# Logits stored by position, offset and head, with one GpSimd product for the V products of two positions

## The chip, the cores and the metric

The kernel runs on one core of one Trainium2 chip (trn2). The core has a matrix engine (TensorE, PE in the profile, with its weight loads as PEld), a vector engine (VectorE, DVE), a scalar engine (ScalarE, ACT), GpSimd (POOL) and SyncE (SP), which here only issues transfers. Data stands in on-chip memory with 128 partitions (SBUF) or in the matrix engine's accumulator banks (PSUM); transfers between them and main memory are called DMAs and are issued by SP, ACT and POOL. The metric is the device time of one execution in microseconds, as the median of the runs.

## What is computed

The reference mixes two branches of the same kind of input, 2048 positions of 640 channels, by a gate for each position.

```python
# branch A: 32 heads of 20 channels, each position looks at 8 positions, 2 apart, behind it
idx = pos[:, None] - off[None, :]                 # off = 0, 2, ..., 14
logits = jnp.einsum("bhsd,bhswd->bhsw", q, kg) * scale
logits = jnp.where(mask[None, None, :, :], logits, -1e9)   # mask = idx >= 0
attn = _softmax(logits, axis=-1)
o = jnp.einsum("bhsw,bhswd->bhsd", attn, vg)
a = o.transpose(...).reshape(B, S, D) @ wo
# branch B: a product in the frequency domain
b = irfft2(rfft2(B_x) * (w_r + 1j * w_i))
g = _sigmoid((x * gate_w).sum(-1, keepdims=True))
return g * a + (1 - g) * b
```

## The kernel before

**Layout.** Position s is 16 p + j: partition p has 16 neighbouring positions. As the heads look back in steps of two, even and odd positions never meet, and every stage runs for a parity `par` (8 even or 8 odd positions of a partition).

**Stages.** The projections to q, k and v (`qkv`) run on PE for each parity and each group of 8 heads; every 128 x 480 result is three exact products in a split format (15 matmuls), copied out by ACT and stored to main memory (`qkvd`). `fold` and `cols` begin the spectral branch on DVE, POOL and PE. `attend(par, h)` makes the attention of 4 heads (80 channels) and one parity, 16 times in all, entirely without PE: it loads kt, q and vt for the 8 positions and the 7 before them. `freq(g)` runs 16 frequency groups: ACT lays out zc, PE multiplies (v, u), DVE adds (ab), PE multiplies again (x, z), ACT issues two transfers that exchange halves (`P<-X`), POOL multiplies P by the weights and adds, DVE finishes (z, s), PE transforms back (g), and ACT copies into zg. `project_even` multiplies the even positions' attention by wo, `spatial` takes the spectral branch back, `project_odd` finishes the odd positions.

**One `attend`** (lines 510 to 570), with the names as they stand in the profile (a suffix 6a is head group 6, first half): for each of four pairs of positions, a product pr of kt and q (1280 elements; on DVE with q first copied by ACT into PSUM, `qbank`; in ten of the sixteen, the last pair's product on POOL) and a sum over the 20 channels into L. Then ACT writes -1e9 into the places before the first position (`mask`, one partition), DVE takes the maximum m, POOL subtracts it, ACT takes the exponential, DVE sums to s and inverts, POOL multiplies. Then, again for each pair, POOL makes the V products pv, one instruction for each position, 640 elements each, and DVE sums over the 8 offsets into o, which is stored.

L is kept as position, head, offset: the 8 offsets of a head lie side by side. The maximum and the sum over the offsets read L densely. A V product takes vt (8 offsets of 80 channels, contiguous), each weight repeated for the head's 20 channels, and writes pv as channel, offset, that is with a step of 8 elements.

**Order.** All instructions are first recorded (`Plan.record`) and then issued in a stored order: `ORDER` (line 204) is a compressed list of places, and `Plan.order` takes the operations out of the recorded list one by one by it. Each engine runs its own instructions in that order and none passes another, so an instruction that waits holds everything behind it on its engine; a DMA issue is such an instruction too. Most tiles stand in rings (`Ring`) with two to eight places, and a tile's first writer waits for the last reader of what stood there.

Nearly all instructions are issued from one line and show as L385 in the profile; they are told apart by the names of their tiles.

Of the kernel before, what the change touches and what calls it, by code (L numbers as in the profile page):

```python
# [12 lines left out]
ALU = mybir.AluOpType  # L13
AX = mybir.AxisListType
# [221 lines left out]


# [18 lines left out]
class Mixer:  # L256
# [253 lines left out]
    def attend(self, par, h, step=4):  # L510

        p, d = self.p, self.qkv_d
        V, A, G, S = p.dve, p.act, p.pool, p.sp
        u, f = 4 * par + h // 2, h % 2
        nm = f"{u}{'ab'[f]}"
# [30 lines left out]
        for square in ((4, 1, 0, 1), (2, 4, 4, 2), (1, 2, 6, 4)):  # L546
            self.mask(L, *square)
        m = self.mr.next(f"m{nm}", 8, 4)
        V.tensor_reduce(out=m, in_=L, axis=AX.X, op=ALU.max)
        G.tensor_sub(L, L, m.unsqueeze(3).broadcast_to([128, 8, 4, 8]))  # L550
        A.activation(out=L, in_=L, func=AF.Exp, scale=SCALE)
        s = self.sr.next(f"s{nm}", 8, 4)
        V.tensor_reduce(out=s, in_=L, axis=AX.X, op=ALU.add)
        V.reciprocal(s, s)
        G.tensor_mul(L, L, s.unsqueeze(3).broadcast_to([128, 8, 4, 8]))
        yield
        for jj in range(0, 8, 2):
            if jj % step == 0:
                o = self.orr.next(f"o{nm}{jj}", 4, HC)[:, 0:step]
            pv = self.pvr.next(f"pv{nm}{jj}", 2, HC, 8)  # L560
            for i in range(2):
                G.tensor_mul(
                    pv[:, i].rearrange("p (h d) r -> p r h d", d=HD),
                    vt[:, jj + i : jj + i + 8].rearrange("p r (h d) -> p r h d", d=HD),
                    L[:, jj + i].rearrange("p h r -> p r h").unsqueeze(3).broadcast_to([128, 8, 4, HD]),
                )
            V.tensor_reduce(out=o[:, jj % step : jj % step + 2], in_=pv, axis=AX.X, op=ALU.add)
            if jj % step == step - 2:
                self.queue("o").dma_start(self.o_d[par][:, jj + 2 - step : jj + 2, HC * h : HC * h + HC], o)
                yield  # L570
# [396 lines left out]
```

## Time and profile before

| What | us |
|---|---|
| median of 3 runs (lowest, highest) | 453.96 (453.48, 454.35) |
| the profiled execution | 455.89 |
| its span, first to last instruction | 454.1 |
| PE busy | 441.2 (97%) |
| DVE busy | 409.8 (90%) |
| POOL busy | 363.9 (80%) |
| ACT busy | 211.9 (47%) |
| the 16 products P<-P,wp on POOL | 35.4 |

The granted clock of PE is 0.996 of full speed. Busy time is the union of an engine's instructions, and matmuls overlap, so PE's share says little by itself; how many matmuls start in a stretch says more. A row of a group gives the engine, the operation, the tile written and those read, the shapes and the count, then the busy time and the mean of one in ns, then the engine's idle time ahead of them and who ended it. A row of the timeline gives the start, the duration, and in brackets the idle time ahead. Neighbouring instructions of POOL and DVE overlap a little in their records, so that what one instruction holds its engine for is read from start to start.

### The profile page before, as it was taken

What the parts mean: (1) busy time and instruction counts of PE and PEld (TensorE: products, weight loads), DVE (VectorE), ACT (ScalarE), POOL (GpSimd) and SP (SyncE); (2) the same over time, 40 slices, a digit from 0 to 9 for tenths busy, and PEclk for the clock granted to TensorE, in tenths of its full rate; (3) what the DMA queues carried; (4) which work ended last, traced back from release to release, by engine and by line L of the source; (5) the groups of instructions that cost most, each with busy time, mean ns of one, the idle gap of its engine ahead of it and who ended that gap; (6) DMA issues with size and microseconds to landing.
All of it is one profiled execution on the core that took longest, in us unless ns stands there. A gap on an engine that the chain in (4) does not pass through costs nothing. (4 is left out here: it accounts for less than half of the span.)

```text
span 454.1 us, 7249 instructions
## 1 busy us (share of the span) xinstructions
PE 441.2 (97%) x2440; PEld 391.8 (86%) x2440; DVE 409.8 (90%) x519; ACT 211.9 (47%) x561; POOL 363.9 (80%) x316
## 2 busy tenths in 40 slices
PE   9999999999999999999998989999989999999996
PEld 6888888888889888899886769998877899999996
DVE  4899999899999999999978989999999997899484
ACT  4723165625226463255356666667554655342110
POOL 1158895899899898988977898976899998889810
PEclk9999999999999999999998999999999999999999
DMA  8998999887968979679979778989883331365932
GB/s 312 401 383 268 340 330 377 305 264 237 272 183 272 340 217 316 181 216 320 303 220 294 240 230 250 297 245 320 258 257 105 85 97 54 118 207 134 296 123 87
DMA packets 73956, 110.75 MB, mean 244 GB/s; under 512 B 21296, under 2 KB 50992, under 8 KB 73920
## 3 DMA queue, kind: packets, MB, share of 16 engines
q1 hardware_dynamic: 40192, 69.32, 46.8%
q10 hardware_dynamic: 32816, 36.97, 26.1%
q0 software_dynamic: 912, 4.00, 2.4%
q8 instruction: 19, 0.31, 0.3%
q14 instruction: 17, 0.14, 0.1%
HBM read 72.51 MB, written 32.84 MB: 232 GB/s over the span
## 5 line engine op out<-in xcount | busy, mean ns | idle before, releaser
L385 PE MATMUL qkv<-w,xo 128*128 128x480 f32 (+1 forms) x480 | 110.6, 385 | 0.0
L385 PE MATMUL qkv<-w,xe 128*128 128x480 f32 (+1 forms) x474 | 104.3, 382 | 0.0
L385 PEld LDWEIGHTS qkv<-w,xe 128*128 128x128 f32 x474 | 89.3, 189 | 15.2 <-ACT xe L385 0.9
L385 PEld LDWEIGHTS qkv<-w,xo 128*128 128x128 f32 x480 | 89.7, 189 | 13.8 <-ACT zg L385 0.2
L385 ACT COPY ev<-qkv 128x480 f32<-128x480 f32 x64 | 34.9, 558 | 48.3 <-PE qkv L385 35.9
L385 PE MATMUL woa<-wo,oT 128*128 128x320 f32 x240 | 47.2, 318 | 0.4 <-ACT oT L385 0.4
L385 PE MATMUL wob<-wo,oT 128*128 128x320 f32 x240 | 46.9, 315 | 0.2 <-ACT ya L385 0.2
L385 POOL TENSOR_TENSOR P<-P,wp 128x963 f32<-128x963 f32 (+1 forms) x16 | 35.4, 2212 | 6.6 <-DMA P<-X 4.0
L385 PEld LDWEIGHTS woa<-wo,oT 128*128 128x128 f32 x240 | 37.7, 188 | 1.1 <-ACT oT L385 0.6
L385 PEld LDWEIGHTS wob<-wo,oT 128*128 128x128 f32 x240 | 37.8, 188 | 0.6 <-ACT ya L385 0.4
L385 POOL TENSOR_TENSOR fx<-fx 128x160 f32<-128x160 f32 (+1 forms) x16 | 12.8, 818 | 24.2 <-DMA fc<-in_t_fc 17.1
L385 POOL TENSOR_TENSOR w<-raw,w 128x480 fp32r<-128x480 f32 (+1 forms) x20 | 24.8, 1262 | 5.3 <-ACT w L385 5.3
L385 ACT CAST oT<-oTp 128x384 fp32r<-128x384 f32 (+1 forms) x32 | 13.4, 427 | 30.9 <-PE oTp L385 17.3
L385 PEld LDWEIGHTS g<-mm,s 128*128 128x128 f32 x150 | 21.0, 190 | 7.1 <-ACT zg L385 5.0
L385 PE MATMUL g<-mm,s 128*128 128x128 f32 x150 | 23.5, 280 | 3.1 <-ACT zg L385 3.0
L385 DVE TENSOR_TENSOR oT<-oTp,oT 128x384 fp32r<-128x384 f32 (+1 forms) x32 | 15.2, 485 | 11.0 <-ACT oT L385 10.7
L385 PE MATMUL oa<-gt,zg 128*128 128x161 f32 (+1 forms) x96 | 24.0, 344 | 0.0
L385 PE MATMUL ob<-gt,zg 128*128 128x161 f32 (+1 forms) x96 | 22.0, 344 | 0.0
L385 PE MATMUL u<-bt,zc 128*128 128x240 f32 (+2 forms) x96 | 21.1, 335 | 0.7 <-DVE ab L385 0.7
L385 PE MATMUL v<-bt,zc 128*128 128x240 f32 (+2 forms) x96 | 21.5, 335 | 0.2
L385 DVE TENSOR_TENSOR fx<-fx 128x642 f32<-128x642 f32 (+2 forms) x24 | 19.2, 798 | 0.7
L385 PEld LDWEIGHTS u<-bt,zc 128*128 128x128 f32 x96 | 16.9, 199 | 2.9 <-PE g L385 0.9
(304 smaller groups left out, 1107.6 us busy)
## 6 DMA issues: line engine op xcount, KB each, us to landing
qkvd<-ev ACTq DMA_DIRECT2D x32, 480.0 KB, 4.8
wp<-in_ws SPq DMA_DIRECT2D x16, 642.0 KB, 5.9
raw<-in_wqkv SPq DMA_DIRECT2D x25, 240.0 KB, 5.9
fx<-in_x SPq DMA_DIRECT2D x8, 641.0 KB, 7.9
ot<-od SPq DMA_DIRECT2D x16, 320.0 KB, 3.9
P<-X ACTq DMA_DIRECT2D x30, 160.5 KB, 4.6
fd<-fx POOLq DMA_DIRECT2D x6, 640.0 KB, 5.6
f<-fd SPq DMA_DIRECT2D x6, 640.0 KB, 6.1
```

Of the source, the lines that this page charges most:

```text
L385: p.dve.memset(w, 0.0)
```

## The change

It does four things.

L is declared as position, offset, head (8, 8, 4). The sum of the K products now writes 32 neighbouring values for each position, and the mask writes the same elements at their new places.

The maximum and the sum over the offsets read L through a view that puts the offsets innermost again, so with a step of 4 elements. The factors m and s of POOL's two operations on L are repeated over the middle axis instead of the last one.

The two V products of a pair of positions become one of 1280 elements. vt is read through a view whose two positions overlap (positions jj to jj+7 and jj+1 to jj+8), and because offset and head now lie side by side, the weights of two positions are one run of 64 values, each repeated 20 times. The 128 instructions become 64.

The stored order is another one. Beside the 64 operations that are gone, 101 stand elsewhere in their engine's list: 8 on PE, 21 on DVE, 48 on ACT, 13 on POOL, 11 on SP (the fewest that turn the one list into the other).

```diff
-        L = self.Lr.next(f"L{nm}", 8, 4, 8)
+        L = self.Lr.next(f"L{nm}", 8, 8, 4)
...
             V.tensor_reduce(
-                out=L[:, jj : jj + 2].rearrange("p j h r -> p j r h"),
+                out=L[:, jj : jj + 2],
                 in_=pr.rearrange("p j r (h d) -> p j r h d", d=HD),
...
-        V.tensor_reduce(out=m, in_=L, axis=AX.X, op=ALU.max)
-        G.tensor_sub(L, L, m.unsqueeze(3).broadcast_to([128, 8, 4, 8]))
+        V.tensor_reduce(out=m, in_=L.rearrange("p j r h -> p j h r"), axis=AX.X, op=ALU.max)
+        G.tensor_sub(L, L, m.unsqueeze(2).broadcast_to([128, 8, 8, 4]))
         A.activation(out=L, in_=L, func=AF.Exp, scale=SCALE)
         s = self.sr.next(f"s{nm}", 8, 4)
-        V.tensor_reduce(out=s, in_=L, axis=AX.X, op=ALU.add)
+        V.tensor_reduce(out=s, in_=L.rearrange("p j r h -> p j h r"), axis=AX.X, op=ALU.add)
         V.reciprocal(s, s)
-        G.tensor_mul(L, L, s.unsqueeze(3).broadcast_to([128, 8, 4, 8]))
+        G.tensor_mul(L, L, s.unsqueeze(2).broadcast_to([128, 8, 8, 4]))
...
-            for i in range(2):
-                G.tensor_mul(
-                    pv[:, i].rearrange("p (h d) r -> p r h d", d=HD),
-                    vt[:, jj + i : jj + i + 8].rearrange("p r (h d) -> p r h d", d=HD),
-                    L[:, jj + i].rearrange("p h r -> p r h").unsqueeze(3).broadcast_to([128, 8, 4, HD]),
-                )
+            w = vt[:, jj : jj + 8]
+            w = bass.AP(tensor=w.tensor, offset=w.offset, ap=[w.ap[0], [HC, 2], [HC, 8], [1, HC]])
+            G.tensor_mul(
+                pv.rearrange("p j c r -> p j r c"),
+                w,
+                L[:, jj : jj + 2].rearrange("p j r h -> p (j r) h").unsqueeze(3).broadcast_to([128, 16, 4, HD]),
+            )
...
-            tensor=ap.tensor, offset=ap.offset + first, ap=[ap.ap[0], [31 * step, n], [32, size], [8, 4], [1, size]]
+            tensor=ap.tensor, offset=ap.offset + 4 * first, ap=[ap.ap[0], [28 * step, n], [32, size], [1, 4], [4, size]]
```

Of the moved operations these are spoken of further on, each in its engine's list:

- ACT: the first copy of q6b to qbank stands ahead of the load of vt6a (it stood behind it); the load of q6b stands two operations and a store later. For the groups 3, 13 and 15 a copy from g to zg that stood behind both loads P<-X stands ahead of them (3) or between them (13, 15). The conversion of the first weight block w0 stands behind two of the five loads issued at the start, where it stood behind all five.
- POOL: the V products of the last pair of 6a and the first of 6b stood split around and behind P11; now 6b's first stands between P11's product and its addition, and 6a's last behind them. The subtraction of the maximum from L5a stands ahead of P12 (it stood behind). The store of zero rows into qkvd stands behind the folds 0 to 2 (it was the first).
- SP: the loads of wo and of the table fct stand earlier, the loads kt5b and kt4b later.

More of the change, by code (lines that the diff above doesn't have):

```diff
@@ L233 @@
-%-FB#M0Qq%ICg_IFP2C48|n56Sm9Um9k2fiPvpqah%)KEUW1~=uV*6=QB*z{Al8lvW9Q;ye=6Tp=v>L79H5IQ5X|z~#8hpnJr+Ga_QrkC4`Rhv7#WXovCK>ybSs8B6l~NOoIP)O5Fr!S
-+}fcYgLx<p#v>wbK=gW?vhdCXZVtgKhsHNHj%~Qolp5+lQ(hjj51#p5_1_2~j|^=(cHJD!9j9&qpZdcxvk%!cXv8;;W{9m%oyJFbB38c|mac656_T8#{}Kg@00
+T>t<81poj4|NsC0{{R31`zHT$$W25WFW#<Ufx}n*nCNU>g@m450OU8>60Nx$Gb89Hl9P1EN2FO}PCCgfdlknEb|e<rai~6a6Gj7t(`^GCh}-Zq0%Nht>e4N4i=1^+C0-pl#~%f%Wq7Mx
+E@|Z1eo=ly=Q4UtCR(E^lMWpq_%;YWs{yxs@@IJ$GIZ6M2sMkb@2|PFhrJngjX(ycmYm3qsU`*g%&K%Bpzz1rHj7QjB>RD3mG!7CtjzFVdyzIKiIG7Cx?{RMlS`CG1mEp0=&j)6A?X*v
@@ new lines @@
+iBB3+!_RL+20IIcT&+?<I{Hrgqd-p9!)D$L8Bdl)ddc(4w2+8neyWg&TsF>LH<+59h;unr(b{%ktR-D2#u5E^kry-q6Y>S!m>>=K>(8HQHp2<eAIpXL7#$Z@U^f@WdcB+21k5EEIWwI%
+H*6Chp!sZ&$dWLX=gg`R+aQxu;q)IVEpvGC<5}IMQLT|Diuz{6fBQEhc@!?`Tx+~3US8`S2WP;S9&%i0=T<`p3;7IL5q&0}hGPc~XpCPfzhMr}10X`ETd0oXV*lg*)BM4I6trbc-Jd%v
+&*_B0BEtIm&X|odr<hDKAagh}+lKEzN9i0mLg`L8ycb?vG0|f}*-{%1ek?c<U9pNjY9g;BQW!^#l?w56#$IAz`Mtq}cNi}^oFNjJ-~CwRGqV*vw0L(V_H^}e3NEp{+=WJ2hO!rv*rWGD
+kZV&Mh6LOOcBdmX-}LYBcGvvrUNE>3OLn}mhv=sy(KQJpeVe6bJ()!^#YHL&6ZN;oeG#?lU<Ab&OHux6U}Su#_~4i!^hMZobA#o&^>sD95+YY;q=4}{hel3tBj;(@h)6uLcP@UhAu8Cm
@@ new lines @@
+&2UMC;dDoLt4>q-+<~U$kRmaaaTuWPWzg?k-Lf5x$#>G2`zWxQGes!@;f1|f=R3HF<3OU9{q)S*Mz=ZH>5=(&hVX#UNzU~Z*sYEg*9WNblIt3?9Jr}2qzi4!CIgTN&3AP?0M4eM4x9qh
+l@*$u3)2=4jA|~}Kee=35WO=}Jg&V-Ywl|$(8F<iSj3meYbfy@V97-A1Bd(*cQuW+h8*#JWjncI!*wkAhI@h+OZ;1iT(*n)Y22HmBUJTl>vf%hJut)QATDe9{mcW(kBl+Oi*M)%ZCjBR
+*H~Jys^=hlj@hm7(#J2allRq9KL?1E@G3D`Y=@Gx3X|AGq9|M?avl^+%!=BC)ESD^GgjkriG^YDKm$nN69I8Qw2U;6<|#a!V7aR%k`27#7$~|onH*T&JOX_LT6PxEVdexeHHl-lBpaz%
+4>zBR!u#c-q!SrNkg6g$Y10;|>1=wDC&&Y`j>e%klG@b`u>G4l9|6a5_9bi05Yp@cwyQs1wY0U}PCkA_uI9{WkAG9N+GfiGhvL+U#$B6AGCa~H5ZsAVE?LU&a7FokIxiIUk8?}24<*Tk
@@ new lines @@
+a^|PjtsVEK6d%$A3g0jIRS_e)PY&IlT3=*PI3fePV)MLuZ}>Hvy)8b^1_|K66)cp`wGMXdbpWOV-AYF79<HMgcv9*V^xErSx#5_<I|w64h>rKqQO%lLON^%<;<QVwlyMU$OwEOz(C>nt
+&d;N!tC|@Q_8PNnoaea>Ie770JC?;M1p)v8_UJY=*CE|IjY-%(O7uueoeDZLyi!QyedJop8`)qgl}kfXknrMa^&2fT+>Ni-ViT68@gr9yr(f!s1UyzwIvn>ij9!Qe61w9Q`xACDqoEo9
++LzxYFEL>8b&{sq1Tmi6DBV4_7pFxLh2>jn;)g-{{;>b~tMy?vyK7wiiPZ6_9p;#YAw64cz%nt;y(Lf~k;rGyL_)GG_KTX5CJq-vk|MnGy6&QGr93_WTDK>3>l}miXm3`24>D#p1e28=
+C17SjrIGwlHk_156UD07b%(<Z%RO4GsVO5Q-1%)<D9UBopX~HyZi>`5tuJ|+azwKzysbl=Knv2``=>KCE5G)l8}mshVfS|P7&^u}1wLxZ&pj#6ty1D0qFTqJ?0S8?q1Ux`!M9XHIic6{
@@ new lines @@
+M6YAMaF58qg}a&XoSdUbNiN~#zM49SwwB6?iDkQS2zx7`XB?KEm)H?9IaKmF_emPS{92_=c7`fuE3nxNi6ftZ#-0tPFlDMs)P>3dp#{|>jtC4alz~g-wQOE9u(#=s_MchYWqTP_hKGsc
+q)-MKaJ*bW;uul9bOhvr{w%<`*cYn>XEcE+xRx32r^z~QS``t8Z^<yGW94kW3|s~N51IaK1&Lb3;!uyEdfT6c`gGp%;R@c|!|)(pFk<w)u5i43rFkc?cuOQ2ccgBznPJxsnlm>b*?4Q#
+-}s!$-?FzKN=k15D~R7CqQJgn-&1LlxV0iC8kVGuTYcFx^PWr8QoEDUKecXWjFuMuwHrAdb?AIiUtmWkEypE+5f@2>n9*-x+Dhn9JxNeh>^6kEOaDx$@YIf_Z{!#=88A1~>Z%hhblCu4
+wSYRS4Xp!CV9T>a|D`*i%p_h%_p&xtiwncj|NWZ0)1owoRY_!+q7r;d`!R2*EMy75mn>U$`~kvOb%We<Ae_U=&HfFU*66$<BsU{1ahiOnlQLWfvO3(MN`N^<lhhUKy0<owWM8CMB?^F<
@@ L235 @@
+Tep_ZV@M0f!s`~1o)A2MydHLre-aXK^oDftbXMtsc<jO%H=p*CT}vsQ$vN;s<Z&4ijQ6X{(OP+UG9_DX10A5Ac^bmo|7Put&0sMkl~H}$eDz$=#1V`^qdDV7D)fvB>MJY`=G3k1|I*)w
+Dvn0C6Yy|3z9S=UJ<-SSR}(%!?;6byKX#n?)SRoIJs%@Bfgp-dhS*04!=GsPqX%=S+9P-`cgqlRJ*%R~fm&@*HJs7A%LgZ-<Tis44fd-c-skR}wORGN2!1s<yn>eS1`vqQj}mN||C?(N
+0T!7G4;V!$#r}{A-<2fLg`#Esa$I`C2`X8!wM)Nk6v0eQgl1e0O7)Rpn)CVw+eK{|uO!g|0=3!gA(}fsUZ<PVSKdgv1Q}lcedN;s
 """
```

36 lines of the change are left out of this document (8 added, 28 removed).

## The prediction

> **What bounds the kernel now.** I read the windows first, since a mean over the span mixes stages, and then the waits of TensorE.
>
> ```profile
> 75.00:100.00 25.00, 25.00 (x116) 21.60 (x115) 23.48 (x23) 11.01 (x29) 23.05 (x19) 1.00 0.85 285
> 125.00:150.00 25.00, 25.00 (x136) 22.19 (x135) 24.83 (x22) 11.70 (x31) 25.00 (x19) 1.00 0.76 242
> 225.00:250.00 25.00, 22.88 (x108) 19.37 (x107) 20.57 (x27) 13.68 (x43) 19.21 (x17) 0.93 0.86 257
> 250.00:275.00 25.00, 22.29 (x129) 18.92 (x128) 22.94 (x37) 16.59 (x49) 22.93 (x19) 1.00 0.78 236
> 325.00:350.00 25.00, 22.50 (x141) 19.48 (x142) 24.26 (x34) 12.21 (x34) 24.27 (x19) 1.00 0.72 217
> 375.00:400.00 25.00, 25.00 (x160) 23.16 (x159) 19.87 (x35) 10.64 (x27) 21.99 (x19) 1.00 0.35 110
> 425.00:454.00 29.00, 25.19 (x176) 24.88 (x175) 16.50 (x40) 3.21 (x8) 7.59 (x9) 1.00 0.43 143
> ```
>
> The columns are the busy microseconds of PE, PEld, DVE, ACT and POOL, then the granted clock and the DMA. Up to 225 us PE is never idle: 116 matmuls of 480 columns in 25 us are one in 0.2155 us. What DVE and POOL do there, the attention in the background, is nearly full too (24.83 and 25.00 of 25), but a microsecond saved in it shortens nothing by itself. Idle PE stands in three of these windows: 2.12, 2.71 and 2.50 us, together 7.3 us. Behind 350 us PE is full again, and the last window holds the end of the program. So the change can win only where PE waits between 225 and 350 us, the stage in which the frequency groups, the last attention heads and the even projections are interleaved.
>
> ```profile
> PE g L385 <- ACT zg L385: 3.0, 5, 1.0
> PE x L385 <- DVE ab L385: 2.0, 1, 2.0
> PE z L385 <- DVE t L385: 1.2, 1, 1.2
> ```
>
> PE waits there for ACT's copy of a group's result into zg (3.0 us in five times), once for DVE's ab (2.0) and once for DVE (1.2). No wait names a V product. POOL counts only through what stands behind the products in its queue.
>
> **The V products.** 128 products of 640 elements become 64 of 1280.
>
> ```profile
> 333.43 2.90 POOL L385 TENSOR_TENSOR pr5b<-kt5b,q5b 128x1280 f32<-128x1280 f32 x1
> 336.28 2.26 POOL L385 TENSOR_TENSOR P<-P,wp 128x963 f32<-128x963 f32 x1
> 344.12 3.91 POOL L385 TENSOR_TENSOR pv6b<-vt6b,L6b 128x640 f32<-128x640 f32 x3
> 347.95 0.62 POOL L385 TENSOR_TENSOR L5a<-L5a,s5a 128x256 f32<-128x256 f32 x1
> L385 POOL TENSOR_TENSOR P<-P 128x321 f32<-128x321 f32 x16 | 12.0, 752 | 1.2
> L385 POOL TENSOR_TENSOR y<-ye 128x321 f32<-128x321 f32 x4 | 3.0, 749 | 0.2
> L385 POOL TENSOR_TENSOR ye<-ho 128x160 f32<-128x160 f32 x8 | 3.6, 472 | 0.0
> L385 POOL TENSOR_TENSOR P<-P,wp 128x642 f32<-128x642 f32 x1 | 1.6, 1550 | 0.0
> ```
>
> Three products take from 344.12 to 347.95, so one holds POOL for 1.277 us and a pair for 2.55. No row shows a product of 1280 elements with a broadcast factor, so I bound it from both sides. The 160 and 321 element rows say that joining two instructions saves 2 x 472 - 749 = 195 ns. The 321 and 642 element rows say that it saves nothing (2 x 752 = 1504 against 1550). The product of 1280 that POOL has already, for K, holds it from 333.43 to 336.28, 2.85 us, which is 0.30 **more** than the pair; but its second factor isn't repeated 20 times as the attention weight is. I take 2.45, a saving of 0.1 per pair, between the first two since their factors are nearer to a halved instruction count than K's. That is 64 x 0.1 = 6.4 us of POOL over the program, with ends of -19 and +12.5 us.
>
> [...]
>
> Little of that is on the path. Between 225 and 350 us some 15 pairs stand in POOL's queue, 1.5 us, and POOL itself often waits for data:
>
> ```profile
> 324.19 2.24 POOL L385 TENSOR_TENSOR P<-P,wp 128x963 f32<-128x963 f32 x1 [1.61 <-DMA P<-X]
> 327.22 0.63 POOL L385 TENSOR_TENSOR L5a<-L5a,m5a 128x256 f32<-128x256 f32 x1
> 339.32 1.39 POOL L385 TENSOR_TENSOR pv6b<-vt6b,L6b 128x640 f32<-128x640 f32 x1
> 341.05 2.29 POOL L385 TENSOR_TENSOR P<-P,wp 128x963 f32<-128x963 f32 x1 [0.34 <-ACT zg L385]
> ```
>
> The product of P12 at 324.19 waits for its transfer whatever stands ahead. From there to the product of P15 at 341.05 POOL has three half pairs of V products, the K product and a subtraction from L5a. In the new order the subtraction is ahead of P12 (0.59 less), but two whole pairs stand there, 4.9 us in place of three halves (3.83): later by 1.07 - 0.59 - 0.34 of idle time = 0.14. So the last groups gain nothing from POOL. I enter 0.3 us for the earlier pairs (between 0 and the 1.5).
>
> **L with the head innermost.** The tile has the same 256 elements. The sums into L write 64 values to other places; the K sums (1479 ns) already write with a gap and take what the V sums (1481 ns, written densely) take. The two POOL operations on L keep their size and lose a factor repeated 8 times in a row: 0 to 0.03 us each, 32 of them, 1 us at most, taken off the saving above. The masks remain four small ACT copies. What differs is the maximum and the sum on DVE: they now read every fourth element, 16 bytes apart.
>
> ```profile
> L385 DVE TENSOR_REDUCE m5a<-L5a 128x32 f32<-128x256 f32 x1 | 0.4, 413 | 0.0
> L385 DVE TENSOR_REDUCE L5a<-pr5a 128x64 f32<-128x1280 f32 x4 | 5.9, 1479 | 0.0
> L385 DVE TENSOR_REDUCE o5b<-pv5b 128x160 f32<-128x1280 f32 x4 | 5.9, 1481 | 1.0 <-POOL pv5b L385 1.0
> ```
>
> From 256 to 1280 elements is 1481 - 413 = 1068 ns, 1.04 ns an element, 267 ns of the 413. DVE reads nothing at such a step in this trace. Bounds: nothing, or every read doubled, +267 ns for each of 32, 8.5 us of DVE. I take nothing for the sum and keep the other end as a rival.
>
> **The moved operations.** In each engine's own list 8 move on PE, 21 on DVE, 48 on ACT, 13 on POOL and 11 on SP. Three places bear on PE's waits.
>
> ```profile
> 220.45 0.34 ACTq L385 DMA_DIRECT2D q6b<-qkvd  x1
> 222.86 0.37 ACTq L385 DMA_DIRECT2D qkvd<-ev  x1
> 228.37 2.20 ACTq L385 DMA_DIRECT2D vt6a<-qkvd  x1
> 230.67 0.30 ACT L385 COPY qbank<-q6b 128x160 f32<-128x160 f32 x1 [2.73 <-POOL pr6a L385]
> 231.00 1.49 DVE L385 TENSOR_TENSOR pr6a<-kt6a,qbank 128x1280 f32<-128x1280 f32 x1 [2.56 <-ACT qbank L385]
> 240.70 0.88 DVE L385 TENSOR_TENSOR ab<-u,vs 128x321 f32<-128x321 f32 x2
> 241.33 0.78 PE L385 MATMUL x<-ab,mm 128*128 128x321 f32 x2 [2.02 <-DVE ab L385]
> ...
> q6b<-qkvd ACTq DMA_DIRECT2D x1, 320.0 KB, 6.5
> ```
>
> First: ACT spends 2.20 us on issuing vt6a's load, the copy of q6b stands behind it, DVE waits 2.56 us for that copy and then has no gap until it makes ab, for which PE waits 2.02 us. The copy now stands ahead of the load. But the load of q6b itself is moved behind the store at 222.86, to about 223.3, and it takes 6.5 us to land, so the copy can run at some 229.8 rather than 230.67. I enter 0.8 us (0 to 2.0).
>
> ```profile
> 251.47 0.47 ACTq L385 DMA_DIRECT2D P<-X  x1
> 252.28 0.48 ACT L385 COPY zg<-g 128x384 f32<-128x384 f32 x1 [0.89 <-DVE o7a L385]
> 252.82 0.71 PE L385 MATMUL g<-mm,s 128*128 128x128 f32 x4 [0.76 <-ACT zg L385]
> 335.20 1.12 ACTq L385 DMA_DIRECT2D P<-X  x2
> 336.36 0.37 ACT L385 COPY zg<-g 128x256 f32<-128x256 f32 x1 [1.23 <-POOL pr5b L385]
> 336.79 0.94 PE L385 MATMUL g<-mm,s 128*128 128x128 f32 x6 [1.03 <-ACT zg L385]
> ```
>
> Second: the two loads that exchange halves of P for a group cost ACT 0.5 to 0.6 us each to issue, and a copy to zg stands behind both. (The page names POOL's pr5b as what ended ACT's wait at 336.36; the two issues just ahead of it, 335.20 to 336.32, fill the same time.) For P3, P13 and P15 the copy now stands ahead of both or between them. PE could win 0.76 at 252.82 and 0.6 at 336.79. The second half of P then lands later by as much, POOL multiplies it later, and DVE and PE wait for that product later on. I enter half, 0.7 us (0 to 1.4).
>
> Third, the start: ACT converts the first weights after two of its load issues instead of five. PE already has raw operands to multiply then, so 0.2 us (0 to 0.5). The store of zero rows goes behind three folds on POOL; the first K load is its only reader near by, and its q load was late anyway. SP's other moves bring wo and the table fct earlier and the loads kt5b and kt4b later; they cost nothing while each lands before its head starts. If that cover is gone, DVE waits for a K tile, some 6 us once.
>
> **Sum.** 0.3 + 0.8 + 0.7 + 0.2 = 2.0 us off. The profiled execution took 455.89 us around a span of 454.1, and would come to 453.9; it lies 1.93 above the median of 453.96, which comes to **451.9 us**.
>
> **Rivals.**
> *Strided reads slow DVE (slower).* By 225 us the heads 0a to 3b and 7a have had 18 maxima and sums, 4.8 us more; until 350 nine more, 2.4. DVE has 4.4 us idle in 225 to 250 to take it up. The other 2.8 come out in the wait for ab, and the four gains shrink to 0.3: 456.5. It decides from about 130 ns an instruction on, when 27 x 0.13 = 3.5 us uses up that slack. For it: DVE has 0.17 us idle in 125 to 150. Against: PE has other matmuls ready while DVE is late. [...]
> *One product of 1280 costs what the K product costs.* By 225 us 36 pairs are 0.30 us longer, 11 us, on a POOL with 0 idle in 125 to 150; the products of P then come late by some 8 us: 462.
> *The gains are hidden.* P's times are set by transfers and PE's waits move elsewhere: 454.0.
>
> **Chances.** Forecast 0.53, its own range 449.0 to 453.0; hidden 0.20; strided reads 0.21; K's rate 0.06. Faster by over 0.2% (0.9 us, about what a measurement of this kernel tells from no change) 0.53, within it 0.20, slower 0.27. The range reaches on the low side to all four terms at their best (1.5 + 2.0 + 1.4 + 0.5 = 5.4 off, 448.5), on the high side 1 us past the strided case (457.5), and leaves K's rate out.
>
> **What would show it.** Right: V products near 2.45 us, maxima near 413 ns, PE's wait for ab under 1.3 us, and its waits for zg under 2.4 in total. Wrong: maxima near 680 ns; V products near 2.85; new PE waits on z or x as large as those that went; a gap of PE ahead of 225 us.

## The result: 1.2 per cent slower

| | before | after |
|---|---|---|
| median | 453.96 us (452.67 to 456.54, 5 runs) | 459.76 us (456.7 to 461.61, 5 runs) |
| ratio, 95% interval | | 1.0117 (1.0074 to 1.0161) |
| profiled execution, its span | 455.89, 454.1 | 461.61, 459.8 |

The forecast was 451.9 us, faster. The time came out on the other side and 2.3 us above the range.

The page of the changed kernel begins with the engines' busy time, its share of the span and the number of instructions:

```profile
PE 442.4 (96%) x2440; PEld 392.2 (85%) x2440; DVE 416.5 (91%) x519; ACT 211.2 (46%) x561; POOL 359.5 (78%) x252
```

The same line of the kernel before, and of e1_dense, a kernel explained below that has the whole change but the strided reads:

```profile
PE 441.2 (97%) x2440; PEld 391.8 (86%) x2440; DVE 409.8 (90%) x519; ACT 211.9 (47%) x561; POOL 363.9 (80%) x316
```

```profile
PE 440.0 (97%) x2440; PEld 390.1 (86%) x2440; DVE 410.4 (91%) x519; ACT 212.4 (47%) x561; POOL 358.9 (79%) x252
```

POOL has 64 instructions less and 4.4 us less work. DVE has the same number of instructions and 6.7 us more, and in e1_dense only 0.6 more. Where the 6.7 come from stands in the groups of the changed kernel (engine, operation, tiles and shapes, then busy microseconds and the mean nanoseconds of one instruction):

```profile
L384 DVE TENSOR_REDUCE s5a<-L5a 128x32 f32<-128x256 f32 x1 | 0.6, 619 | 0.0
L384 DVE TENSOR_REDUCE m5a<-L5a 128x32 f32<-128x256 f32 x1 | 0.6, 609 | 0.0
...
L384 DVE TENSOR_REDUCE L5a<-pr5a 128x64 f32<-128x1280 f32 x4 | 5.9, 1476 | 0.0
```

The maximum that took 413 ns takes 609, the sum that took 414 takes 619, and 32 such instructions at about 0.2 us are 6.4 us. The sum into L, which now writes densely, stays at 1476 ns (1479 before): nothing is won in exchange.

What PE waits for, longest in total first (total microseconds, times, longest one), in the changed kernel:

```profile
PE g L384 <- DVE s L384: 3.1, 2, 2.7
PE x L384 <- DVE ab L384: 2.1, 2, 1.5
PE z L384 <- DVE s L384: 1.6, 1, 1.6
PE warmed L384 <- DVE warm L384: 1.1, 1, 1.1
PE qkv L384 <- ACT xe L384: 1.0, 1, 1.0
PE g L384 <- ACT zg L384: 0.7, 2, 0.6
```

The waits for ACT's copies into zg, 3.0 us before, are down to 0.7, as was meant. In their place stand waits for DVE: 3.1 + 2.1 + 1.6 us, where before it was 2.0 for ab and 1.2 for t. And the windows that answer to those shown of before (busy PE, PEld, DVE, ACT, POOL, then the granted clock):

```profile
225.00:250.00 25.00, 22.72 (x113) 19.22 (x112) 24.77 (x27) 13.36 (x42) 22.63 (x16) 1.00 0.87 243
250.00:275.00 25.00, 23.32 (x137) 19.86 (x136) 24.52 (x42) 17.74 (x56) 23.93 (x18) 1.00 0.93 297
...
325.00:350.00 25.00, 21.46 (x138) 18.77 (x135) 22.53 (x32) 11.93 (x33) 21.42 (x12) 0.98 0.85 248
```

Between 225 and 250 us DVE was busy for 20.57 us of 25; now for 24.77. That is the line to remember: the idle time of DVE in that stretch, on which the price of the strided reads in the prediction relied, isn't there in the changed kernel.

**By stage.** The table counts PE's instructions in both traces and gives the microseconds between the same numbers in PE's list, for the stretches that begin at these times in the kernel before. It is worked out from the start of each matmul; 8 of PE's instructions are moved, so a few tenths mean little.

```
                  0   12  130-225  225-262  262-300  300-330  330-352   352 to the end
before         11.0 117.9    95.0     36.5     38.6     30.0     22.0    102.1
after          11.5 119.0    95.9     35.3     37.2     31.5     26.8    101.7
e1_dense       12.2 119.0    95.5     33.1     38.1     30.2     21.5    101.7
```

The change loses 2.5 us up to 225 us, wins 2.6 from 225 to 300, and loses 6.3 from 300 to 352. With dense reads the win from 225 to 300 is 3.9, and the last loss is gone. Some 1.7 us of these wins are the granted clock in the profiled execution of the kernel before: behind PE's wait of 2.02 us at 241.33 it is at half for 3.41 us, which the eighth figure of a window (after POOL's busy time) shows as (0.25 + 0.09) x 5 us:

```profile
240.00:245.00 5.00, 3.67 (x13) 3.24 (x14) 4.06 (x7) 1.70 (x4) 4.92 (x4) 0.75 0.91 320
245.00:250.00 5.00, 4.90 (x26) 4.13 (x25) 4.21 (x9) 4.13 (x15) 2.25 (x4) 0.91 1.02 286
```

The span of e1_dense's profile, without such a fall, is 1.7 us shorter than that of before, though their medians can't be told apart.

**The place where most is lost** in this execution, as the timeline of the changed kernel shows it (start, duration, engine, operation; in brackets the idle time ahead and what ended it):

```profile
337.22 0.47 ACTq L384 DMA_DIRECT2D P<-X  x1
...
337.56 2.25 POOL L384 TENSOR_TENSOR P<-P,wp 128x963 f32<-128x963 f32 x1 [1.63 <-DMA P<-X]
...
340.58 2.71 POOL L384 TENSOR_TENSOR pv6b<-vt6b,L6b 128x1280 f32<-128x1280 f32 x1
...
344.93 2.23 POOL L384 TENSOR_TENSOR P<-P,wp 128x963 f32<-128x963 f32 x1 [1.64 <-DMA q4b<-qkvd]
...
347.24 0.75 POOL L384 TENSOR_TENSOR P<-P 128x321 f32<-128x321 f32 x1
...
348.02 0.89 DVE L384 TENSOR_TENSOR s<-P,z 128x321 f32<-128x321 f32 x2 [0.33 <-POOL P L384]
348.66 1.40 PE L384 MATMUL g<-mm,s 128*128 128x128 f32 x6 [2.71 <-DVE s L384]
```

PE waits 2.71 us for DVE's s, DVE for POOL's sum of P, POOL for a transfer. (The line names q4b's load; the last half of P, issued at 337.22, takes 7.5 us to land, to about the same time.) In e1_dense everything up to here is about 2.3 us earlier and the same chain is short:

```profile
339.74 2.26 POOL L384 TENSOR_TENSOR P<-P,wp 128x963 f32<-128x963 f32 x1 [0.37 <-DMA q4b<-qkvd]
...
343.36 0.89 DVE L384 TENSOR_TENSOR s<-P,z 128x321 f32<-128x321 f32 x2
...
344.12 0.74 PEld L384 LDWEIGHTS g<-mm,s 128*128 128x128 f32 x6 [0.65 <-ACT zg L384]
```

The transfers of P took up to 7.5 us to land in 326 to 342 us of the changed kernel, with a median of 5.5, and up to 4.6 with a median of 3.3 in e1_dense. e10_more_elements below, with dense reads, has long ones too (in 318 to 346 us a median of 4.1, as in the change, where e1_dense has 3.4), so that part is not put down to the strides. Behind the gap the granted clock is at 0.50 for 6.83 us; that is told at the end. It isn't the main loss: three of the changed kernel's five executions have a mean clock of 0.998 or more and still took 456.7 to 459.76 us, where the eight of e1_dense at 0.999 or more took 451.66 to 454.82.

### The profile page after: what moved, and what is told of

Read it like the earlier page. It is cut to its first block, busy times and chain, and to the rows that moved or that the text cites. A ratio compares the mean times of both kernels' runs of the same rounds, so it can differ in the third digit from the quotient of the medians.

```text
span 459.8 us, 7192 instructions
## 1 busy us (share of the span) xinstructions
PE 442.4 (96%) x2440; PEld 392.2 (85%) x2440; DVE 416.5 (91%) x519; ACT 211.2 (46%) x561; POOL 359.5 (78%) x252
## 5 line engine op out<-in xcount | busy, mean ns | idle before, releaser
L384 PEld LDWEIGHTS g<-mm,s 128*128 128x128 f32 x150 | 22.0, 198 | 7.4 <-issue 3.0
L384 PE MATMUL g<-mm,s 128*128 128x128 f32 x150 | 24.5, 288 | 3.9 <-DVE s L384 3.1
L384 PE MATMUL oa<-gt,zg 128*128 128x161 f32 (+1 forms) x96 | 25.7, 365 | 0.0
L384 PE MATMUL u<-bt,zc 128*128 128x240 f32 (+2 forms) x96 | 20.0, 322 | 0.7 <-DVE ab L384 0.7
L384 ACT CAST w<-raw 128x480 fp32r<-128x480 f32 (+1 forms) x30 | 17.1, 595 | 7.2 <-POOL fx L384 3.6
```

What stands on the lines that cost most here:

```text
L384: p.dve.memset(w, 0.0)
```

## The experiments

Four theories: **A**, the strided reads cost by the time that they take on DVE. **B**, the new order costs. **C**, the joined product costs by when it ends. **D**, the joined product costs about 1 per cent in an order made for two short ones, and the new order makes up for it. Every ratio is to the kernel before on the same chip, five rounds each, with its 95% interval.

### Taking the change apart

Three parts, each there or not: the reads (dense, strided), the V product (two, one), the order (of before, new). The changed kernel with dense reads; of its two edits the one of the maximum is shown:

```diff
-V.tensor_reduce(out=m, in_=L.rearrange("p j r h -> p j h r"), axis=AX.X, op=ALU.max)
+V.tensor_reduce(out=m, in_=L.rearrange("p j r h -> p j (r h)").rearrange("p j (a b) -> p j a b", b=8), axis=AX.X, op=ALU.max)
```

The sum is edited in the same way. This is **e1_dense** (one product, new order):

> The changed kernel, but the maximum and the sum of each head group read L densely, eight neighbours at a time (so over other elements than the offsets; the masked places hold -30 instead of -1e9). Everything else, the one product of 1280 and the new order, stays. Theory A (the reads with a step of 16 bytes cost 0.2 us each on DVE, 32 times): maxima and sums back at about 413 ns, DVE 6.4 us less busy than in the changed kernel, time at or under the kernel before, 450 to 455. Theory B (the new order is what costs): 458 or more. Theory C (the joined product costs by when it ends, not by its length): 457 or more.

454.37 us, 1.0002 (0.997 to 1.0034).

**e2_strided** is the kernel before (two products, old order) with reads at a step of four elements:

```diff
-V.tensor_reduce(out=m, in_=L, axis=AX.X, op=ALU.max)
+V.tensor_reduce(out=m, in_=L.rearrange("p j h r -> p j (h r)").rearrange("p j (a b) -> p j b a", b=4), axis=AX.X, op=ALU.max)
```

> The kernel before with its own order and its two V products, but the maximum and the sum of each head group read L with a step of 4 elements (over other elements than the offsets; the masked places hold -30). Theory A: maxima and sums near 612 ns, DVE 6.4 us busier, time 456 to 460. Theories B and C: 454 within 1.

455.35 us, 1.0013 (0.9988 to 1.0039), between the two expectations.

**e3_old_order** is the changed kernel with the order of before, the joined product in the place of the first of its pair:

```diff
-ORDER = (new)
+ORDER = (that of before, without the second product of each pair)
```

> The changed kernel in the stored order of the kernel before (each joined product where the first of its pair stood). Theory A: 457 to 463, no better than the changed kernel, since DVE keeps the longer reads. Theory B: 452 to 455.

459.15 us, 1.0110 (1.0068 to 1.0153). That is in theory A's range, but not for A's reason, as e5_dense_old below shows: with dense reads this order is as slow.

**e4_new_order** is the kernel before with the new order, both products of a pair where the joined one stands:

```diff
-ORDER = (that of before)
+ORDER = (new, with the second product of each pair right behind the first)
```

> The kernel before, dense reads and two V products, in the stored order of the changed kernel (the second product of a pair right behind the first). Theory A: 452 to 456. Theory B: 458 or more, the cost comes with the order alone.

457.32 us, 1.0057 (1.0029 to 1.0085), between the two expectations.

**e5_dense_old** is e1_dense in the order of before, **e6_strided_new_order** is e2_strided in the new order of e4_new_order.

> The joined product alone: dense reads (over other elements than the offsets; the masked places hold -30), the order of the kernel before. Theory A (strided reads cost, the joined product doesn't): 453 to 455. Theory D (the joined product costs about 1% in an order made for two short ones, and the new order makes up for that): 457 to 460.

457.81 us, 1.0109 (1.0073 to 1.0145).

> Strided reads (over other elements than the offsets; the masked places hold -30) and two V products, in the new order. If the costs of strided reads (+0.13% in the old order) and of the new order (+0.57%) add: 457 to 458.5. If the reads cost what they cost with the joined product in the new order (1.15%): 461 to 463.

457.57 us, 1.0101 (1.0063 to 1.0140).

Together, the ratios to before:

| reads | two products, old order | one, old order | two, new order | one, new order |
|---|---|---|---|---|
| dense | 1 (before) | 1.0109 (e5) | 1.0057 (e4) | 1.0002 (e1) |
| strided | 1.0013 (e2) | 1.0110 (e3) | 1.0101 (e6) | 1.0117 (the change) |

The parts don't add up. The joined product by itself costs 1.1 per cent, the new order by itself 0.6, both together nothing: D is right as far as that goes, and the 101 moves belong to the joined product. The strided reads cost nothing that can be told in the old order, 0.4 with the two products in the new one (the intervals of e4 and e6 overlap), and 1.15 in the change itself. So in the change the reads are what makes it slower than before, but the same reads were almost free in the kernel that I had the profile of.

### Why the joined product costs in the old order

In 20 of the 64 pairs other POOL work stood between the two products of the old order. **e9_second_place** leaves everything of e5_dense_old but puts the joined product where the *second* one stood:

```diff
-ORDER = (that of before, without the second product of each pair)
+ORDER = (that of before, without the first product of each pair)
```

> The order of before, one product for two positions, dense reads as in e5_dense_old (1.0109), with one difference: the joined product stands where the second product of its pair stood, not the first. In 20 of the 64 pairs other POOL work (halves of P, K products, steps on L, the other head's products) stood between the two. Theory D, place: in the old order the joined product costs because it pushes that work back by one product, 1.3 us; at the second's place it no longer does, and only the sums of the first position come later: 1.000 to 1.004. Theory D, time: the product of 1280 itself is what costs (its duration, or its sum that can start only behind both positions), wherever it stands: 1.008 to 1.013.

454.5 us, 1.0012 (0.998 to 1.0044): it is the place. POOL's timeline of the kernel before has half a pair ahead of the sum of P:

```profile
250.17 2.24 POOL L385 TENSOR_TENSOR P<-P,wp 128x963 f32<-128x963 f32 x1
252.36 1.37 POOL L385 TENSOR_TENSOR pv7b<-vt7b,L7b 128x640 f32<-128x640 f32 x1
253.63 0.76 POOL L385 TENSOR_TENSOR P<-P 128x321 f32<-128x321 f32 x1
```

and that of e5_dense_old the whole of it, with DVE and PE waiting behind:

```profile
255.50 2.52 POOL L383 TENSOR_TENSOR pv7b<-vt7b,L7b 128x1280 f32<-128x1280 f32 x1
...
257.87 0.77 POOL L383 TENSOR_TENSOR P<-P 128x321 f32<-128x321 f32 x1
...
258.67 0.89 DVE L383 TENSOR_TENSOR s<-P,z 128x321 f32<-128x321 f32 x2 [2.58 <-POOL P L383]
...
259.31 1.19 PE L383 MATMUL g<-mm,s 128*128 128x128 f32 x4 [2.72 <-DVE s L383]
```

In e9_second_place the sum of P starts right behind the product of P, and the V product comes last:

```profile
249.22 2.23 POOL L383 TENSOR_TENSOR P<-P,wp 128x963 f32<-128x963 f32 x1
251.53 0.75 POOL L383 TENSOR_TENSOR P<-P 128x321 f32<-128x321 f32 x1
...
253.66 2.55 POOL L383 TENSOR_TENSOR pv7b<-vt7b,L7b 128x1280 f32<-128x1280 f32 x1
```

The joined instruction holds POOL for 2.52 us without a break where half a pair held it for 1.37, and the sum of P, which stood between the two halves, starts 4.56 us behind the start of its product in e5_dense_old, where it was 3.46 in the kernel before (2.31 in e9_second_place). The 20 places mended this way do in the old order what the 101 moves do. C, in the form that the longer product costs by its own end, falls with it: the product is the same here as in e5_dense_old, and the sum of the first position starts later still.

### Why the strided reads cost

**e10_more_elements** asks whether it is the time on DVE alone. It is e1_dense, but the maximum and the sum read 448 elements densely in place of 256:

```diff
-V.tensor_reduce(out=m, in_=(256 elements of L), axis=AX.X, op=ALU.max)
+x = bass.AP(tensor=L.tensor, offset=L.offset, ap=[L.ap[0], [8, 32], [0, 2], [1, 7]])
+V.tensor_reduce(out=m.rearrange("p a b -> p (a b)"), in_=x, axis=AX.XY, op=ALU.max)
```

> The kernel of e1_dense (1.0002: dense reads, one product, new order), but maximum and sum read 448 elements densely in place of 256 (seven of each eight, twice). By 1.04 ns an element each takes some 610 ns, as the strided ones do. The values are not the maxima and sums of the reference. Theory A, time on DVE: the 0.2 us on each of 32 instructions is all that the strided reads cost, so this is as slow as the changed kernel: 1.009 to 1.015. Rival: strided reads cost by hindering other engines' access to SBUF, or the readers of L: 0.998 to 1.003 with dense reads of the same length.

458.83 us, 1.0105 (1.0067 to 1.0143), as slow as the change. Its groups have

```profile
L384 DVE TENSOR_REDUCE m5a<-L5a 128x32 f32<-128x448 f32 x1 | 0.6, 614 | 0.0
```

and its windows

```profile
225.00:262.00 37.00, 33.77 (x172) 28.33 (x171) 36.65 (x45) 22.07 (x68) 34.17 (x24) 1.00 0.89 268
330.00:352.00 22.00, 18.32 (x111) 15.44 (x110) 20.20 (x29) 10.56 (x28) 18.89 (x12) 0.95 0.78 243
```

614 ns without any stride, and the trace looks like that of the change: DVE busy for 36.65 of 37 us. So A is shown for this order: 0.2 us on each of 32 DVE instructions costs this much, and no hindrance of other engines by the strided access is needed to explain it. (The kernels with dense reads over other elements don't compute the reference's values; e7_turned_new below reads densely, does compute them, and in the same order is at 1.0020.) The same window in the kernel before, in the change and in e1_dense:

```profile
225.00:262.00 37.00, 33.86 (x168) 28.43 (x166) 31.08 (x40) 21.86 (x67) 29.37 (x25) 0.95 0.82 246
```

```profile
225.00:262.00 37.00, 33.74 (x173) 28.30 (x172) 36.68 (x44) 21.43 (x68) 33.72 (x24) 1.00 0.91 271
```

```profile
225.00:262.00 37.00, 35.30 (x183) 29.72 (x182) 35.56 (x45) 23.32 (x73) 33.11 (x23) 1.00 0.91 274
```

In the old order DVE has 5.9 us idle there. With the new order PE does 15 matmuls more in the same time; some 8 of these are the 1.7 us of lost clock in the execution of before, at 0.2 us each, the rest are the order's. DVE has to keep up (35.56), and 1.44 us of slack are left. The strided reads use them up, and PE falls back to 173 matmuls. By the table by stage this stretch takes 35.3 us in place of 33.1, 2.2 of the 7.4 us between the spans of the two profiles. Whether the order gives or takes the slack is what the two next kernels test.

**e13_second_strided** has both edits of the change, in the order of e9_second_place:

> The two edits of the change (L with the head innermost, strided maximum and sum; one product for two positions) in the order of before, the joined product at the place of the second of its pair: e9_second_place (1.0012) with strided reads. Theory A, 0.2 us on each of 32 instructions of DVE wherever they stand: 1.009 to 1.015. Theory A with slack: the strided reads cost by what else the order has put on DVE's and PE's chain (they cost 0.1 per cent with two products in the old order, 1.15 with one in the new), and the old order with the joined product out of the way leaves them that slack: 1.000 to 1.006. Then it is the new order that makes DVE's time count.

456.54 us, 1.0053 (1.0028 to 1.0078): 0.4 per cent above e9_second_place, a third of what the reads cost in the change. The time is in the range of the part of A with slack, near its upper end, though the two intervals overlap. In 225 to 262 us PE makes 179 matmuls here, and 178 in e9_second_place, the same order with dense reads:

```profile
225.00:262.00 37.00, 34.32 (x179) 28.91 (x178) 36.55 (x47) 22.97 (x72) 34.53 (x25) 1.00 0.86 269
```

```profile
225.00:262.00 37.00, 33.98 (x178) 28.64 (x177) 34.20 (x45) 23.09 (x72) 32.59 (x25) 1.00 0.87 262
```

DVE had 2.8 us idle there, the reads take up most of it, and PE loses nothing in this stretch. Where the 0.4 per cent come from isn't shown.

**e14_late_old** is the changed kernel with the old order from about 262 us on:

> The changed kernel, with the order of before from operation 2057 of 3592 on, from about 262 us. In its profile PE lost 4.7 us against before in 330 to 352 us, a gap of 2.98 us and 6.83 us at half the granted clock behind it. Theory late: the new order of the last groups, with DVE late, makes that gap; the old one there has none with the same strided reads (e3_old_order: 22.9 us for that stage): 1.003 to 1.008. Theory everywhere: DVE is late by then whatever the order, and the time comes out at the end all the same: 1.009 to 1.014.

457.95 us, 1.0092 (1.0072 to 1.0112). The gap in the last groups is gone from its profile (the stretch from 330 to 352 takes 22.0 us as before), but the time is still high, as the theory that has the loss everywhere expects, at its low end: the large gap of the profiled execution is a small part of the loss. Where the rest comes out is not shown stage by stage: this profile has a wait of 2.1 us for ACT's xe at the start, where the change's has 1.0, and a mean granted clock of 0.996 (0.993 in the change).

**e11_max_only** and **e16_sum_only** leave one of the two reads dense:

> New order, one product, the maximum strided, the sum dense (it reads other elements than the offsets): half of the 32 long instructions. If their cost adds up one by one, half of the 1.15 per cent: 1.004 to 1.008. If there is slack up to a point, as the prediction's rival had it (it decides from about 130 ns an instruction, here 100 on average): 0.998 to 1.003. If what costs is the maximum's place in the chain sums, mask, maximum, subtraction, exponential: 1.009 to 1.014.

456.64 us, 1.0034 (1.0002 to 1.0066).

> The other half of e11_max_only (1.0034): the sum strided, the maximum dense (it reads other elements than the offsets), one product, new order. If the strided instructions' costs add up, the two halves together make the 1.0117 of the changed kernel: 1.006 to 1.010. If there is slack up to a point (some 0.13 us an instruction, as the prediction's rival worked out), this costs as little as the other half: 0.999 to 1.005.

456.12 us, 1.0044 (1.0014 to 1.0075). The halves make 0.78 per cent together, the whole 1.17 with an interval of 0.74 to 1.61. One half came out between the two expectations, the other in that of a slack up to a point. Whether they add up can't be told from these numbers. Both halves are above the kernel before, but their intervals overlap with that of e1_dense.

### Is there a version that beats both?

**e7_turned_new** keeps L as before (dense reads) and lets POOL's normalizing product write the weights with the head innermost into a second tile, from which the joined product reads:

```diff
-G.tensor_mul(L, L, s.unsqueeze(2).broadcast_to([128, 8, 8, 4]))
+W = self.Wr.next(f"W{nm}", 8, 8, 4)
+G.tensor_mul(W.rearrange("p j r h -> p j h r"), L, s.unsqueeze(3).broadcast_to([128, 8, 4, 8]))
```

> The whole computation. L stays position, head, offset, with dense reads on DVE; GpSimd's last product on L writes the attention weights into a second tile as position, offset, head, from which the joined product of two positions is made; the new order. Theory A: maxima and sums at 413 ns, the writing product at 0.63 to 0.9 us, 453 to 456. If a write with a step of 16 bytes costs GpSimd what the read costs DVE: the writing product at 0.83 or more, 455 to 457.

455.62 us, 1.0020 (0.9991 to 1.0050). **e8_turned_old** is the same in the old order, the joined product in the first place:

> The same with the order of the kernel before. Theory A: 453 to 456. Theory D: 457 to 460, as in the run with dense reads and the old order.

456.73 us, 1.0062 (1.0035 to 1.0089), between the two expectations.

**e12_old_front** is e7_turned_new with the order of before for the first 1136 operations, because the new one idles PE there; **e15_turned_mixed** has the order of e9_second_place up to about 115 us and the new one behind. The windows from 12 to 130 us of before, of the change and of e12_old_front:

```profile
12.00:130.00 118.00, 118.00 (x543) 101.84 (x542) 112.52 (x120) 50.38 (x127) 91.92 (x88) 1.00 0.89 308
```

```profile
12.00:130.00 118.00, 117.37 (x538) 100.72 (x537) 111.52 (x118) 49.34 (x125) 88.62 (x77) 1.00 0.90 306
```

```profile
12.00:130.00 118.00, 118.00 (x543) 101.83 (x542) 110.40 (x118) 50.20 (x126) 89.84 (x77) 1.00 0.89 307
```

> e7_turned_new (dense reads, weights written with the head innermost by POOL, one product, new order; 1.0020), but with the order of before for the first 1136 of 3592 operations, up to about 130 us. Theory B, by pieces: the new order loses about 1.1 us in the start and 1.1 us between 12 and 130 us, and wins behind 225; without the loss 450.5 to 452 us against 454, 0.992 to 0.998, the first version below the kernel before. If what the front loses is only work done earlier, given back later: 1.000 to 1.004.

454.09 us, 1.0001 (0.9967 to 1.0035). The idle time of PE in 12 to 130 us is gone, and the profiled execution had the shortest span of all, 450.9 us, but the runs don't bear out a gain.

> The dense kernel of e7_turned_new (L with the offset innermost; POOL writes the normalized weights with the head innermost; one product), with the pieces of order that were the shortest each: the one of e9_second_place up to 115 us, the new one behind. By the stages of e9, e7 and e12: 0.993 to 0.999. If PE is at its floor apart from gaps that come and go with the transfers: 0.999 to 1.003, as e12_old_front.

455.46 us, 1.0011 (0.9979 to 1.0042). No version that was tried beats the kernel before by what can be measured; five with one product for two positions (e1, e7, e9, e12, e15) can't be told from it, three of them (e7, e12, e15) with the whole computation of the reference.

## Why the prediction was wrong

**The step that failed** is "I take nothing for the sum and keep the other end as a rival", on the strided maximum and sum. The bounds were 0 and 267 ns an instruction; the rows say 196 (609 against 413) and 205 (619 against 414), near the far end. For this step of 16 bytes that is 0.2 us for 256 elements, about 0.78 ns for each; no run has another step, so the reason isn't shown. The prediction had the case as a rival and gave it 0.21.

**A second step stood behind it**: "DVE has 4.4 us idle in 225 to 250 to take it up". That slack was read off the old order's trace, and the same change replaced that order. In the changed kernel DVE is busy for 24.77 of those 25 us. The rival's condition, from about 130 ns an instruction on, was therefore worked out with slack that the new order spends elsewhere; in the old order, where the slack is, the same reads cost 0.1 per cent, which can't be told from nothing (e2). The 130 ns don't come out of its own numbers either: 4.4 us over 27 instructions are 163 ns. "PE has other matmuls ready while DVE is late" fell too: PE's waits for DVE's s and ab are 6.8 us.

**The rival's price**, 456.5, was 3.3 us short of 459.76 although its reads were dearer than the real ones, mostly because it let 4.4 us of that slack pay for them; 0.3 us more are the gains that it left in. Without slack, 27 instructions at the measured 0.2 us are 5.4 us, and 454.37 (e1_dense) and 5.4 make 459.8. That this meets the time so well is in part luck, since the same reads cost less in e6 and e13.

**The gains** didn't come: e1_dense measures them by themselves, 1.0002, nothing, where the sum had 2.0 us. They were read off a profiled execution that lies 1.93 us above the median and holds the fall of the clock at 242 us, and taken off the median. Whether an execution without that fall has the same waits isn't known, as none was profiled.

Of the four terms of the sum:

*V products, 0.3 us from a saving of 0.1 a pair.* The size was right. Two of the sixteen heads, before and after:

```profile
L385 POOL TENSOR_TENSOR pv2a<-vt2a,L2a 128x640 f32<-128x640 f32 x8 | 11.2, 1470 | 0.6 <-DVE o1b L385 0.4 <-DVE o2a L385 0.2
...
L385 POOL TENSOR_TENSOR pv5a<-vt5a,L5a 128x640 f32<-128x640 f32 x8 | 10.6, 1369 | 0.1
```

```profile
L384 POOL TENSOR_TENSOR pv2a<-vt2a,L2a 128x1280 f32<-128x1280 f32 x4 | 11.0, 2752 | 2.3 <-DVE o2a L384 1.9 <-DVE o1b L384 0.5
...
L384 POOL TENSOR_TENSOR pv5a<-vt5a,L5a 128x1280 f32<-128x1280 f32 x4 | 10.2, 2559 | 3.2 <-DVE o5a L384 2.1 <-DVE o6b L384 1.0
```

0.05 and 0.10 us a pair, and POOL's busy time is 4.4 us lower in all; the product itself takes 2.56 to 2.75 us in these rows, not the 2.45 of the prediction. What the term left out is the other side of joining, the place: in the old order it costs 1.1 per cent (e5), and the new order's moves (e1), or the second place (e9), are needed to pay for it. The prediction counted that only for P12 to P15, as 0.14 us.

*q6b's copy, 0.8 us.* In e1_dense PE's single wait of 2.0 us for ab is gone, so the step was right by itself; in the change 2.1 us stand there again, in two waits. *The copies to zg, 0.7 us.* Those waits fell by 2.3 us, more than the 1.4 at best, but waits for DVE's s came in their place. *The start, 0.2 us to the good.* It went the other way: the same number of PE's instructions takes 0.5 us longer up to 12 us and 1.1 longer from there to 130 (the table by stage), with a new wait of 1.0 us for ACT's xe (1.4 in e1_dense). The prediction asked for "a gap of PE ahead of 225 us" as a sign of being wrong, and there it is.

## What to carry to other kernels

Slack belongs to an order: the 4.4 us that DVE was idle in 225 to 250 us of the old order were 0.23 in the new one, so when a change replaces the order that the profile was taken of, price a dearer instruction as if that engine were full. Two instructions joined into one hold their queue without a break (POOL's product here 2.5 us), so list what stood between them, and try the joined one in the place of the second (1.0012 here, against 1.0109 in the place of the first). Before a layout is turned for one reader's sake, count what every other reader of it pays per element (about 0.78 ns here on DVE).

## What the runs showed of the hardware

**Reads at a step of 16 bytes on DVE** cost 0.75 of an element's time on top: 609 ns for 256 elements, while 256 dense ones take 413 and 448 dense ones 614, which is (614 - 413) / 192 = 1.05 ns for a dense element. **On POOL writing at such a step costs little**: the normalizing product that writes W in e7_turned_new takes 679 ns in the mean of the 16 heads, where the kernel before has 635 and e1_dense 646.

**A gap of PE was paid twice.** Behind the wait of 2.71 us in the changed kernel the granted clock falls:

```profile
345.00:350.00 5.00, 2.22 (x12) 1.66 (x10) 2.80 (x5) 1.31 (x5) 4.92 (x3) 0.89 0.45 146
350.00:355.00 5.00, 4.43 (x14) 3.58 (x14) 5.00 (x6) 1.28 (x3) 4.00 (x4) 0.50 0.00 0
355.00:360.00 5.00, 5.00 (x30) 4.38 (x29) 4.27 (x3) 2.09 (x7) 4.93 (x2) 0.93 0.46 126
```

5 x (0.11 + 0.50 + 0.07) = 3.4 us of full clock are lost, more than the wait itself, and 14 matmuls are made in 5 us where the next 5 us have 30. e10_more_elements has 0.96, 0.50 and 0.85 in the same three windows. A wait of 1.82 us at 344.82 in e11_max_only is followed by a fall, one of 1.85 at 241.84 in e9_second_place isn't; a window of each:

```profile
345.00:350.00 5.00, 4.43 (x18) 3.72 (x18) 5.00 (x6) 1.19 (x3) 4.92 (x4) 0.66 0.11 44
```

```profile
240.00:245.00 5.00, 3.16 (x17) 2.81 (x18) 4.80 (x8) 2.25 (x6) 3.92 (x2) 1.00 1.02 333
```

So waits of 1.8 and 2.7 us were followed by a fall in some cases, and no length is shown to be safe: waits of up to 1.5 us in the changed kernel's 225 to 250 us left the clock at 1.00, one of 1.85 us did too, and one of 1.82 us didn't. The fall lasts 3.41 us in the kernel before (242.52 to 245.93 us) and 6.83 in the change (348.90 to 355.73). What decides whether a wait is followed by one isn't shown.

Single executions of one kernel lie several microseconds apart, and in some kernels the ones with the lower mean clock are the longer ones: in e1_dense 453.9 us at 1.0 and 457.49 at 0.993. In e14_late_old they aren't: 458.93 us at 1.0 and 457.64 at 0.996.

**What stays open.** Why the new order with two short products costs 0.6 per cent (e4) wasn't followed further. It goes with the clock: its three executions at 1.0 took 453.58 to 454.74 us, the nine below that 456.07 to 458.92; why the clock falls so often there isn't known. Nor was it tried what makes the transfers of P slower in 326 to 345 us in some executions.
